# Where the scaling and the store of finished results stand around a value loop

## The chip, the cores and the metric

One core of a Trainium2 chip. The time is device microseconds of one execution; medians are over several executions on one chip. PE is the matrix engine, DVE the vector engine, ACT the scalar engine; SP issues the loads. A DMA has landed at the last of the 16 counts that the trace shows for it on its semaphore.

## The reference

Attention of one query a head over 4096 keys, for 8 x 32 heads of width 128, in bf16:

```python
scores = jnp.einsum('bhqd,bhkd->bhqk', q, k) * q.shape[-1] ** -0.5   # Sq = 1, Skv = 4096
attn = softmax(scores)
return jnp.einsum('bhqk,bhkd->bhqd', attn, v)
```

K and V are 268 MB each and are read once: 537 MB of loads against 0.07 MB of results.

## The kernel before

Eight heads make a tile, 32 tiles in all. A tile's K and V are 8.39 MB each and share three slots of SBUF. DVE multiplies K by the query and adds halves (lines 185, 188, 193), PE sums further against an identity (205), DVE reduces to scores (217), ACT takes exps (249), and PE multiplies the weights with V in a loop of its own (first and last matmuls line 274, the turns 288). ACT copies that result (344), PE folds it into `op` (360). In every second tile `op` is scaled by ACT (369), and after every fourth scaling a 16 KB store goes out from ACT (375). The loads are issued from SP (151).

```python
OB = 4          # results in one store
LOOP = 6        # matmuls in a turn of the value loop
kv_pool = ctx.enter_context(tc.tile_pool(name="kv_pool", bufs=SLOTS))   # SLOTS = 3
...
def values_loop(t):
    ...
    with tc.tile_critical() as loop:
        for i in range(EDGE): one(i, start=(i == 0), stop=False)        # L274
        with pe.While(...):
            for i in range(LOOP): pe.matmul(av, ...)                    # L288
            pe.reg_add(rw, rw, LOOP * nw); pe.reg_add(rv, rv, LOOP * nv)
        for i in range(NV - EDGE, NV): one(i, start=False, stop=(i == NV - 1))
    loops.append(loop)
...
def finish_of(n):
    s, u = divmod(n, OB)
    ...
    nc.scalar.activation(out=stages[s][:, u, :], in_=ops.pop(n)[:], func=ACT.Copy,
                         scale=rzs.pop(n)[:, 0:1])                      # L369
    last = s == NQ // OB - 1
    if u == OB - 1 or (last and u == OB - 2):
        lo = u if (last and u == OB - 1) else 0
        nc.scalar.dma_start(o_n[s, :, lo : u + 1, :], stages[s][:, lo : u + 1, :])   # L375
...
for t in range(NT):
    ...
    product(t, 0, Q);          sum_over_d(t, 0)
    ...
    product(t, Q, 2 * Q);      sum_over_d(t, 1);  scores_of(t, 0)
    product(t, 2 * Q, 3 * Q);  sum_over_d(t, 2);  scores_of(t, 1)
    if t > 2 and t % R == 1:
        recip_of(n)
        finish_of(n)
    product(t, 3 * Q, C);      sum_over_d(t, 3);  scores_of(t, 2)
    if loop:                                   # tiles 1 to 29
        values_loop(t - 1)
        load("k", t + 1);  load("v", t)
    ...
    scores_of(t, 3);  weights_of(t)
    if t > 0:
        copy_of(t - 1)
        ...
        result_of(t - 1)
```

The value loop is a section that is entered as a whole. In the trace of this kernel PE waits, ahead of the loop's first matmul, not only for the weights and V that it reads: in tiles 9, 17 and 25 its instruction records there wait on 13 semaphores, all eight that the DMAs count among them, and so the store's too. The wait on the store's semaphore was over at 402.09, 718.60 and 1035.73 us, 0.02 to 0.03 us behind the store's landing (402.06, 718.58, 1035.71), and the loop's first matmul had waited 10.25, 5.06 and 5.54 us.

Of the kernel before, what the change touches and what calls it, by code (L numbers as in the profile page):

```python
# [16 lines left out]
R = 2  # L17
OB = 4
# [7 lines left out]
def kernel(  # L26
# [7 lines left out]
    nc = tc.nc  # L34
# [15 lines left out]
    NQ = NT // R  # L50
# [95 lines left out]
    def load(kind, t):  # L146
        src = k_t if kind == "k" else v_t
        buf = kv_pool.tile([P, C, D], BF16, name=f"{kind}t", tag="kv")
        c0 = 0
        for n in cuts.get((kind, t), [C]):  # L150
            dma = nc.sync.dma_start(buf[:, c0 : c0 + n, :], src[t, :, c0 : c0 + n, :])
            behind_loop(dma)
            c0 += n
            if kind == "k" and t == 0 and c0 == n:
                nc.sync.dma_start(q_all[:], q_n)
        assert c0 == C
        loads[kind, t] = buf
# [3 lines left out]
    def q_prep(t):  # L161
        x, p0 = divmod(t * G, P)
        qh = ps_q.tile([G, D], F32, name="qh", tag="qp")
        nc.tensor.matmul(  # L164
            qh[:], lhsT=ident[:, p0 : p0 + G], rhs=q_all[:, x, :], start=True, stop=True
        )
        qg = q_pool.tile([G, D], BF16, name="qg", tag="qg")
        nc.scalar.activation(out=qg[:], in_=qh[:], func=ACT.Copy)  # L168
        qp = ps_q.tile([P, D], F32, name="qp", tag="qp")
        nc.tensor.matmul(qp[:], lhsT=heads[:].rearrange("g h x -> g (h x)"), rhs=qg[:], start=True, stop=True)  # L170
        qb = q_pool.tile([P, 1, D], BF16, name="qb", tag="qb")
        nc.scalar.activation(out=qb[:, 0, :], in_=qp[:], func=ACT.Copy)  # L172
        qbs[t] = qb
# [6 lines left out]
    def product(t, lo, hi):  # L180
        kt = loads["k", t]
        qb = qbs[t]
        for c0 in range(lo, hi, MC):
            part = kt[:, c0 : c0 + MC, :]
            nc.vector.tensor_tensor(  # L185
                out=part, in0=part, in1=qb[:].to_broadcast([P, MC, D]), op=ALU.mult
            )
            nc.vector.tensor_tensor(  # L188
                out=part[:, :, 0 : D // 2], in0=part[:, :, 0 : D // 2],
                in1=part[:, :, D // 2 : D], op=ALU.add,  # L190
            )
            if width_of(t, c0 // UC) < D // 2:
                nc.vector.tensor_tensor(  # L193
                    out=part[:, :, 0 : D // 4], in0=part[:, :, 0 : D // 4],
                    in1=part[:, :, D // 4 : D // 2], op=ALU.add,
                )
# [3 lines left out]
    def sum_over_d(t, u):  # L200
        kt = loads["k", t]
        ps = ps_s.tile([P, UC, DS], F32, name="ps", tag="ps")
        n = width_of(t, u) // DS
        for s in range(n):
            nc.tensor.matmul(  # L205
                ps[:], lhsT=ident[:],
                rhs=kt[:, u * UC : (u + 1) * UC, s * DS : (s + 1) * DS],
                start=(s == 0), stop=(s == n - 1),
            )
        sums[t, u] = ps  # L210
# [3 lines left out]
    def scores_of(t, u):  # L214
        if u == 0:
            scs[t] = sc_pool.tile([P, C], F32, name="sc", tag="sc")
        made = nc.vector.tensor_reduce(  # L217
            out=scs[t][:, u * UC : (u + 1) * UC], in_=sums.pop((t, u))[:], axis=AX.X, op=ALU.add
        )
        if u == NU - 1:  # L220
            behind_loop(made)
# [4 lines left out]
    def weights_of(t):  # L226
        sc = scs.pop(t)
        pmax = small.tile([P, 1], F32, name="pmax", tag="pmax")
        nc.vector.tensor_reduce(out=pmax[:], in_=sc[:], axis=AX.X, op=ALU.max)  # L229
        spread = small.tile([P, TB], F32, name="spread", tag="spread")  # L230
        nc.vector.tensor_scalar(  # L231
            out=spread[:], in0=same[:], scalar1=pmax[:, 0:1], scalar2=-scale,
            op0=ALU.add, op1=ALU.mult,
        )
        nmax = small.tile([P, 1], F32, name="nmax", tag="nmax")
        nc.vector.tensor_reduce(  # L236
            out=nmax[:], in_=spread[:], axis=AX.X, op=ALU.min, apply_transpose=True
        )
        bias = small.tile([P, G], F32, name="bias", tag="bias")
        nc.vector.tensor_scalar(  # L240
            out=bias[:], in0=own[:], scalar1=nmax[:, 0:1], scalar2=None, op0=ALU.add
        )
        w = w_pool.tile([P, C // CB, G, CB], BF16, name="w", tag="w")
        if t % R == 0:
            esums[t // R] = small.tile([P, R, G], F32, name="esum", tag="esum")
        esum = esums[t // R]
        sc_g = sc[:].rearrange("p (i m) -> p i m", m=CB)
        for g in range(G):
            nc.scalar.activation(  # L249
                out=w[:, :, g, :], in_=sc_g, func=ACT.Exp, bias=bias[:, g : g + 1], scale=scale,  # L250
                accum_out=esum[:, t % R, g : g + 1],
            )
        ws[t] = w
        if t == NT - 1:
            nc.gpsimd.tensor_copy(
                out=w_last[:, :, RG - G : RG].rearrange("p m g -> p g m"),
                in_=w[:, (C - LAST) // CB, :, :],
            )
# [67 lines left out]
    def norm_of(n):  # L326
        zp = ps_z.tile([RG, 1], F32, name="zp", tag="zp")
        nc.tensor.matmul(
            zp[:], lhsT=esums.pop(n).rearrange("p r g -> p (r g)"), rhs=ones[:],
            start=True, stop=True,  # L330
        )
        zps[n] = zp

    def recip_of(n):
        rzs[n] = small.tile([RG, 1], F32, name="rz", tag="rz")
        nc.vector.reciprocal(out=rzs[n][:], in_=zps.pop(n)[:])  # L336
# [3 lines left out]
    def copy_of(t):  # L340
        comb = o_pool.tile([P, CB, D], BF16, name="comb", tag="comb")
        av = avs.pop(t)[:].rearrange("p (m d) -> p m d", d=D)
        n = AG if t < LT else P
        nc.scalar.activation(out=comb[0:n, :, :], in_=av[0:n, :, :], func=ACT.Copy)  # L344
        combs[t] = comb
# [19 lines left out]
    def finish_of(n):  # L365
        s, u = divmod(n, OB)
        if u == 0:
            stages[s] = o_pool.tile([RG, OB, D], BF16, name="stage", tag="stage")
        nc.scalar.activation(  # L369
            out=stages[s][:, u, :], in_=ops.pop(n)[:], func=ACT.Copy, scale=rzs.pop(n)[:, 0:1]  # L370
        )
        last = s == NQ // OB - 1
        if u == OB - 1 or (last and u == OB - 2):
            lo = u if (last and u == OB - 1) else 0
            nc.scalar.dma_start(o_n[s, :, lo : u + 1, :], stages[s][:, lo : u + 1, :])  # L375
# [5 lines left out]
    with tc.manual_schedule(engines={E.PE, E.DVE, E.Activation, E.SP}):  # L381
        q_prep(0)
        for t in range(NT):
            loop = 0 < t <= LT
            v_last = t >= NT - 2
            n = t // R - 1
            if not loop:
                if t + 1 < NT:
                    load("k", t + 1)
                load("v", t)  # L390
            product(t, 0, Q)
            sum_over_d(t, 0)
            if t + 1 < NT:
                q_prep(t + 1)
            product(t, Q, 2 * Q)
            sum_over_d(t, 1)
            scores_of(t, 0)
            product(t, 2 * Q, 3 * Q)
            sum_over_d(t, 2)
            scores_of(t, 1)  # L400
            if t > 2 and t % R == 1:
                recip_of(n)
                finish_of(n)
            product(t, 3 * Q, C)
            sum_over_d(t, 3)
            scores_of(t, 2)
            if loop:
                values_loop(t - 1)
                load("k", t + 1)
                load("v", t)  # L410
            if v_last:
                values_of(t - 1, 0, C)
            scores_of(t, 3)
            weights_of(t)
            if t > 0:
                copy_of(t - 1)
                if t % R == 0:
                    norm_of(n)
                result_of(t - 1)
        values_of(NT - 1, 0, C // 2)  # L420
        norm_of(NQ - 1)
        recip_of(NQ - 1)
        values_of(NT - 1, C // 2, C - LAST)
        copy_of(NT - 1)
        result_of(NT - 1)
        finish_of(NQ - 1)


# [28 lines left out]
```

## Time and profile before

| | before |
|---|---|
| median of 3 runs | 1283.41 us (1279.34 to 1284.44) |
| span of the profiled run | 1280.6 us |
| loads' packets, share of 16 DMA engines | 98.0% |
| DVE, PE busy | 81%, 60% |
| stores that stand ahead of a value loop | 3 (tiles 9, 17, 25) |
| these stores, from issue to landing | 19.0, 14.0, 14.6 us |

The DMA share of 98.0% says that the loads are nearly the limit here. It does not say what the missing 2% are. In the list of issues on SP, the distance from one K load to the next gives the time of a tile: where it is longer than its neighbours, the trace holds a stall, and the waits of the engines at that time give its cause. The prediction shows these views.

### The profile page before, as it was taken

Reading aid. Unit: us, or ns where it says so; the run is one execution under the profiler, and the core shown is the slowest. Engines: PE = TensorE matmul, PEld = TensorE weight load, DVE = VectorE, ACT = ScalarE, POOL = GpSimd, SP = SyncE. Lnnn points to the kernel's source line nnn. Section 1 sums busy time; section 2 is a strip of 40 time slices with the busy share of each in tenths; the row PEclk is TensorE's granted clock in tenths of the full one; section 3 lists DMA queues with packets and bytes.
Section 4 is the critical chain, followed back from the end, with each engine's and each line's share of the span. In section 5 each row is a group of like instructions: output and inputs, shape, how many; then the busy total and the mean of one; then the engine's idle time right before and its main releaser. Section 6 shows DMA issues by size and latency. Waiting matters only on the chain. (4 is left out here: it accounts for less than half of the span.)

```text
span 1280.6 us, 11028 instructions
## 1 busy us (share of the span) xinstructions
PE 766.2 (60%) x3067; PEld 287.8 (22%) x3067; DVE 1040.6 (81%) x588; ACT 172.4 (13%) x625; POOL 3.3 (0%) x18
## 2 busy tenths in 40 slices
PE   2265567655574556765557655577555665557756
PEld 0021122221221122222222222222221222222222
DVE  5997888888986788888898787987889869788784
ACT  0111011111011101111101111111110111101111
POOL 0000000000000000000000000000000000000000
PEclk9577888777886788877788677887778877788867
DMA  9999999999999899999999999999999999999997
GB/s 426 428 393 426 428 424 441 414 434 428 440 430 396 356 430 414 426 428 437 426 426 437 416 393 426 422 428 439 416 436 434 432 402 394 426 426 427 428 447 304
DMA packets 11433, 537.33 MB, mean 420 GB/s; under 512 B 1808, under 2 KB 2064, under 8 KB 2320
## 3 DMA queue, kind: packets, MB, share of 16 engines
q1 hardware_dynamic: 11072, 536.94, 98.0%
q8 instruction: 14, 0.23, 0.1%
q10 hardware_dynamic: 336, 0.07, 0.0%
q14 instruction: 11, 0.09, 0.0%
HBM read 536.94 MB, written 0.07 MB: 419 GB/s over the span
## 5 line engine op out<-in xcount | busy, mean ns | idle before, releaser
L185 DVE TENSOR_TENSOR kt<-kt,qb 128x8192 bf16<-128x8192 bf16 x128 | 565.2, 4416 | 70.0 <-DMA kt<-in_k_dram 58.5
L205 PE MATMUL ps<-kt,ident 128*128 128x512 bf16 x792 | 261.0, 480 | 419.9 <-DVE kt L193 369.7
L288 PE MATMUL av<-vt,w 128*32 x1740 | 426.5, 397 | 4.7
L188 DVE TENSOR_TENSOR kt<-kt 128x4096 bf16<-128x4096 bf16 x128 | 293.4, 2292 | 4.4
L288 PEld LDWEIGHTS av<-vt,w 128*32 x1740 | 173.0, 99 | 263.9 <-issue 123.2
L205 PEld LDWEIGHTS <-ident 128*128 128x128 bf16 x792 | 84.5, 113 | 571.2 <-issue 523.2
L217 DVE TENSOR_REDUCE sc<-ps 128x64 f32<-128x512 f32 x128 | 88.0, 687 | 140.8 <-PE ps L205 140.8
L249 ACT ACTIVATE w<-sc,bias 128x256 bf16<-128x256 f32 x256 | 126.4, 494 | 518.5 <-DVE bias L240 518.5
L193 DVE TENSOR_TENSOR kt<-kt 128x2048 bf16<-128x2048 bf16 x58 | 71.0, 1225 | 2.0
L274 PE MATMUL av<-vt,w 128*32 128x512 bf16 x116 | 47.3, 501 | 34.0 <-DMA out_dram<-stage 15.8
L344 ACT ACTIVATE comb<-av 32x512 bf16<-32x512 f32 (+1 forms) x32 | 18.8, 587 | 345.2 <-PEq L278 337.5
L249 ACT ACTIVATION_READ_ACCUMULATOR w<-sc,bias 128x1 f32 x256 | 47.7, 186 | 0.0
L360 PE MATMUL op<-comb,pick 32*16 32x128 bf16 (+1 forms) x128 | 12.1, 213 | 25.8 <-ACT comb L344 25.8
L274 PEld LDWEIGHTS av<-vt,w 128*32 128x32 bf16 x116 | 7.1, 101 | 74.1 <-issue 73.7
L369 ACT ACTIVATE stage<-op,rz 16x128 bf16<-16x128 f32 x16 | 5.7, 358 | 132.4 <-DVE rz L336 132.0
L168 ACT ACTIVATE qg<-qh 8x128 bf16<-8x128 f32 x32 | 8.5, 267 | 99.4 <-PE qh L164 99.4
L360 PEld LDWEIGHTS <-pick 32*16 32x16 bf16 (+1 forms) x128 | 8.8, 83 | 32.9 <-issue 32.5
L316 PE MATMUL av<-vt,w 128*32 128x512 bf16 x191 | 15.4, 418 | 0.0
L164 PE MATMUL qh<-q_all,ident 128*8 128x128 bf16 x32 | 7.1, 221 | 13.1 <-DMA q_all<-in_q_dram 13.1
L229 DVE TENSOR_REDUCE pmax<-sc 128x1 f32<-128x256 f32 x32 | 13.4, 420 | 1.1
L170 PE MATMUL qp<-qg,heads 8*128 8x128 bf16 x32 | 6.8, 213 | 11.4 <-ACT qg L168 11.4
L172 ACT ACTIVATE qb<-qp 128x128 bf16<-128x128 f32 x32 | 8.9, 278 | 9.6 <-PE qp L170 9.6
(29 smaller groups left out, 47.9 us busy)
## 6 DMA issues: line engine op xcount, KB each, us to landing
kt<-in_k_dram SPq DMA_DIRECT2D x7, 4096.0 KB, 21.2
kt<-in_k_dram SPq DMA_DIRECT2D x2, 2048.0 KB, 15.2
vt<-in_v_dram SPq DMA_DIRECT2D x1, 4096.0 KB, 32.1
vt<-in_v_dram SPq DMA_DIRECT2D x1, 2048.0 KB, 36.6
vt<-in_v_dram SPq DMA_DIRECT2D x1, 1024.0 KB, 38.7
vt<-in_v_dram SPq DMA_DIRECT2D x1, 512.0 KB, 38.2
vt<-in_v_dram SPq DMA_DIRECT2D x31, 24.1
kt<-in_k_dram SPq DMA_DIRECT2D x28, 26.4
```

Source lines behind the costliest of these rows:

```text
L185: nc.vector.tensor_tensor(out=part, in0=part, in1=qb[:].to_broadcast([P, MC, D]), op=ALU.mult)
L188: nc.vector.tensor_tensor(out=part[:, :, 0 : D // 2], in0=part[:, :, 0 : D // 2], in1=part[:, :, D // 2 : D], op=ALU.add,)
L193: nc.vector.tensor_tensor(out=part[:, :, 0 : D // 4], in0=part[:, :, 0 : D // 4], in1=part[:, :, D // 4 : D // 2], op=ALU.add,)
L205: nc.tensor.matmul(ps[:], lhsT=ident[:], rhs=kt[:, u * UC : (u + 1) * UC, s * DS : (s + 1) * DS], start=(s == 0), stop=(s == n - 1),)
L217: made = nc.vector.tensor_reduce(out=scs[t][:, u * UC : (u + 1) * UC], in_=sums.pop((t, u))[:], axis=AX.X, op=ALU.add)
L229: nc.vector.tensor_reduce(out=pmax[:], in_=sc[:], axis=AX.X, op=ALU.max)
L249: nc.scalar.activation(out=w[:, :, g, :], in_=sc_g, func=ACT.Exp, bias=bias[:, g : g + 1], scale=scale, accum_out=esum[:, t % R, g : g + 1],)
L274: pe.matmul(av, lhsT=wf[:, i * nw : (i + 1) * nw], rhs=vf[:, i * nv : (i + 1) * nv], **how)
L288: pe.matmul(av, lhsT=wf[:, bass.ds(ow + i * nw, nw)], rhs=vf[:, bass.ds(ov + i * nv, nv)], start=False, stop=False,)
L316: nc.tensor.matmul(avs[t][j * AG : (j + 1) * AG, :], lhsT=w[:, i, :, :], rhs=vt[:, c0 : c0 + CB, :], start=(i < TG), stop=(j not in group[ ...
L344: nc.scalar.activation(out=comb[0:n, :, :], in_=av[0:n, :, :], func=ACT.Copy)
L360: nc.tensor.matmul(ops[n][:], lhsT=pick[0:e, m, r, :], rhs=comb[0:e, m, :], start=(r == 0 and m == 0), stop=(r == R - 1 and m == CB - 1),)
```

## The change

The intent: a store must not stand in the way of the value loop. Scaling goes behind the exps of the tile and so behind the loop in the program; the store goes behind the copy of the loop's result.

```diff
-        nc.scalar.activation(
+        made = nc.scalar.activation(
             out=stages[s][:, u, :], in_=ops.pop(n)[:], func=ACT.Copy, scale=rzs.pop(n)[:, 0:1]
         )
+        behind_loop(made)
+
+    def store_of(n):
+        s, u = divmod(n, OB)
         last = s == NQ // OB - 1
 ...
             if t > 2 and t % R == 1:
                 recip_of(n)
-                finish_of(n)
             product(t, 3 * Q, C)
 ...
             weights_of(t)
+            if t > 2 and t % R == 1:
+                finish_of(n)
             if t > 0:
                 copy_of(t - 1)
+                if t > 2 and t % R == 1:
+                    store_of(n)
 ...
         finish_of(NQ - 1)
+        store_of(NQ - 1)
```

## The prediction

> **What bounds the kernel now.** I read the page first, for the load queue; then the order of the load issues; then, where that order breaks, who waits for whom; last the neighbourhood of one break in time.
>
> The page says that the loads are the resource in use nearly all the time, while DVE is 81% and PE 60% busy:
>
> ```profile
> PE 766.2 (60%) x3067; PEld 287.8 (22%) x3067; DVE 1040.6 (81%) x588; ACT 172.4 (13%) x625; POOL 3.3 (0%) x18
> ...
> q1 hardware_dynamic: 11072, 536.94, 98.0%
> ```
>
> That alone would say "nothing on ACT can matter". But 98.0% of 1280.6 us leaves some 26 us, and it is worth asking where they lie. The issues of loads on the SP queue, in time order (K and V of a tile alternate), around the seventh to eleventh tile:
>
> ```profile
> 331.59 0.33 SPq L151 DMA_DIRECT2D kt<-in_k_dram  x1
> 353.62 0.33 SPq L151 DMA_DIRECT2D vt<-in_v_dram  x1
> 370.44 0.33 SPq L151 DMA_DIRECT2D kt<-in_k_dram  x1
> 392.53 0.33 SPq L151 DMA_DIRECT2D vt<-in_v_dram  x1
> 419.36 0.33 SPq L151 DMA_DIRECT2D kt<-in_k_dram  x1
> 441.32 0.33 SPq L151 DMA_DIRECT2D vt<-in_v_dram  x1
> 458.13 0.33 SPq L151 DMA_DIRECT2D kt<-in_k_dram  x1
> ```
>
> The normal distance from K to K is 38.9 us (370.44 - 331.59 = 38.85; 458.13 - 419.36 = 38.77). It is 22.0 us from K to V and 16.8 us from V to K. From 370.44 to 419.36 it is 48.92. In the whole list only two other distances stand out: 691.93 to 735.79 (43.86) and 1008.47 to 1053.01 (44.54). Over 38.9 these are 10.0, 5.0 and 5.6 us: 20.6 us in all, and no later tile catches up (458.13, 497.06, 536.01 go on at 38.8 to 39.0).
>
> What holds a K load is the end of the value loop, whose slot it takes; and the loop started late. The waits view gives PE's reasons:
>
> ```profile
> PE av L274 <- DMA out_dram<-stage: 15.8, 2, 10.2
> PE av L274 <- issue: 11.8, 27, 0.6
> ...
> PE av L274 <- DMA kt<-in_k_dram: 5.1, 1, 5.1
> ```
>
> 27 loops start 0.4 to 0.6 us after the matmuls ahead of them; three wait 10.2, 5.6 and 5.1 us. Two are put down to the store of the results. The third (at 719.04) is put down to a K load, but I hold it for the store too: in the trace the last part of that store landed at 718.58 and the K load at 718.78, and the list of waits in the built program has the store's semaphore ahead of that loop and not this K load's. In time:
>
> ```profile
> 383.10 7.00 ACTq L375 DMA_DIRECT2D out_dram<-stage  x1
> ...
> 390.63 1.86 PE L205 MATMUL ps<-kt,ident 128*128 128x512 bf16 x4 [6.71 <-DVE kt L193]
> ...
> 402.75 1.03 PE L274 MATMUL av<-vt,w 128*32 128x512 bf16 x2 [10.25 <-DMA out_dram<-stage]
> ...
> 422.25 0.69 DVE L217 TENSOR_REDUCE sc<-ps 128x64 f32<-128x512 f32 x1 [11.50 <-PE ps L205]
> ```
>
> PE is free at 392.5; the loop starts at 402.75; it ends at 419.4; behind it PE makes the sums that DVE then waits 11.5 us for (2.0 us in a usual tile, at 373.40). So the ring is: loop, sums on PE, DVE's products, sums, loop. It closes in 38.9 us and has no room, so a late loop is a late everything. The data queue runs dry meanwhile: 319 and 262 GB/s in 408 to 416 and 416 to 424 us, 426 to 434 usual.
>
> [...] the branch into each loop has a chain of such waits on all DMA semaphores, [...] the store included, though the loop reads nothing of it. [...] a 16 KB store is 80 packets, 5 on each of 16 engines, and a load packet takes 2.42 us; [...] the stores land 14.0 and 14.6 us after their issue (19.0 for the first, whose issue alone took 7.00). [...] Here 0.32 us of issue against 14 us to landing. [...] The packet records show a load of 8.39 MB ending every 19.34 us when the queue is full, 434 GB/s[...].
>
> **The change part by part.** Nothing is added or removed: PE, DVE and SP keep their order, and ACT only moves two things.
>
> Scaling (16 ACTIVATEs of 358 ns): from ahead of the loop to behind the eight exps of the same tile. In the loop tiles ACT then waits some 10 us for the loop's end (10.87 us idle ahead of the copy at 370.51), so 0.36 us there is hidden. In the last odd tile, which has no loop, the chain of waits runs exps (to 1268.66), copy, result: there 0.36 us is on the path. Cost +0.4.
>
> Stores (three of 16 KB in loop tiles): from ahead of the loop to behind the copy that follows it. The built program drops the store from that loop's counts[...]. Gain at the present loops: 10.0 + 5.0 + 5.6 = 20.6 us. The new deadline: counted from a V issue S, the loop ends at S + 16.8, the copy 0.65 later, so the store is issued at about S + 17.6 and lands at S + 31.6 to 32.2, or S + 36.6 if the first one again takes 7 us to issue. The next loop starts at S + 38.9 + 0.6 = S + 39.5. Margin 7 us, 2.9 us for the first: no wait.
>
> A 7 us issue on ACT would sit ahead of the query copy that PE waits for (373.55 in a usual tile): about 3.5 us late. PE's second sums end then at about K issue + 10.2, while DVE asks for them at K issue + 11.5 (381.93 - 370.44). Hidden, with 1.3 us to spare.
>
> What does not come back: the loads. With a full queue two loads cost 38.7 us at best, and in the undisturbed stretches K lands every 39.05 us (523.63 to 718.90 in five tiles) to 39.17 (840.24 to 1036.07), a little more than the ring's 38.9. DVE's wait for K grows from 0.54 us behind the first stall to 2.95 ahead of the second, and from 1.52 to 3.6 ahead of the third, while its wait for PE shrinks to 0.5 to 0.9. So the stalls gave the ring no slack but gave DVE slack against the loads. Without them the loads come to bind: up to 15 tiles at 0 to 0.2 us, some 1.5 us (estimate), and some 0.7 us more at the end, where the last V pieces have been only about 2 us ahead of their matmuls. Sum: -20.6 + 0.4 + 1.5 + 0.7 = -18.0 us. From the median of 1283.4 that is 1265.4; I say 1265.
>
> **The rivals.** (a) The wait moves: the store lands behind the start of the next loop. For it: [...] the 19.0 us landing leaves only 2.9 us. Against it: the two other landings leave 7. If only the first is late by some 3 us, 1268; if all three waits move whole, 1284. (b) The loads bind alone: the gain is only the load time lost. For it: 98.0% busy. Counting how much longer than 19.34 us each load at the three breaks took, from the packet records, gives 10.3 + 5.8 + 4.8 = 20.9 us, of which some 2 us are the usual spread (0.23 us a load): 18.8 us, so even then 1265. The two ways of counting agree, which narrows the range. (c) More than the stalls is won, say because loops at other odd tiles also waited for the scaling. Against it: they start as promptly as the rest, within 0.6 us. It would need 25.7 us to pass 2%, more than the three waits hold. (d) Nothing: the stores' wait overlapped a wait for data. Against it: no V landing stands near 402.75 or 1036.06, and the issue distances jump by the same amounts.
>
> **Range and chances.** The steps of the sum carry 2 to 3 us of doubt (loads), the first store 3, and the runs of the kernel before spread from 1279.3 to 1284.4. So 1261 to 1270. 2% would be 1257.7, beyond the 20.6 us on offer: faster 0.03; slower 0.02; within 2% 0.95.
>
> **What would show it.** Right: no K to K distance over 40 us but for the first tiles; no wait of the loop's first matmul over 1 us; issues of stores about 0.7 us behind the K issue; landings of 12 to 19 us; DVE waits for K that climb to about 4 us and stay, and a load queue near 99%. Wrong: a loop wait of some us one tile later, which names the store (rival a); or prompt loops with K to K distances of 39.3 and more (the loads took the gain). A median under 1261 would mean the loads keep up better than I read.

With the cuts goes the reason that it gave for landings of about 14 us; the landings themselves (19.0, 14.0 and 14.6 us) are measured, and the new deadline uses these alone. That the next loop waits for a store that now stands ahead of it was my assumption: the runs show such waits only for stores issued in the loop's own tile (the kernel before, `e2_early_ahead`, `e4_twice_ahead`, `e9_before_loop30`). What the text says of waits in the program can be seen in the traces. Ahead of the loop at 719.04 the wait on the store's semaphore was over at 718.60, behind its landing at 718.58, and the one on the K load's semaphore at 718.71, ahead of that load's landing at 718.78; so this K load was not what the loop waited for. In the changed kernel the loop at 392.92 starts ahead of the store's issue at 409.67.

## The result, and the profile after

| | before | after |
|---|---|---|
| median | 1282.97 us (4 runs, 1279.34 to 1284.44) | 1261.68 us (4 runs, 1261.61 to 1261.99) |
| ratio | | 0.9839 (95% interval 0.9818 to 0.9859) |
| span of the profiled run | 1280.6 us | 1260.2 us |
| K to K at tiles 9, 17, 25 | 48.92, 43.86, 44.54 us | 39.20, 38.97, 38.90 us |

A ratio is the mean time of one kernel's runs over that of the other's of the same rounds, so it is not quite the ratio of the medians quoted. The time of 1261.68 us lies in the range of 1261 to 1270, near its lower end, and within 2% of before.

The issues of loads after the change, on the SP queue, at the place where the stall of 10 us was:

```profile
370.32 0.33 SPq L151 DMA_DIRECT2D kt<-in_k_dram  x1
392.40 0.33 SPq L151 DMA_DIRECT2D vt<-in_v_dram  x1
409.52 0.33 SPq L151 DMA_DIRECT2D kt<-in_k_dram  x1
431.55 0.33 SPq L151 DMA_DIRECT2D vt<-in_v_dram  x1
448.35 0.33 SPq L151 DMA_DIRECT2D kt<-in_k_dram  x1
```

K to K is 39.20 and 38.83 us; V to K is 17.1 us at the place where it was 26.8. The same stretch on all engines, cut to the scaling, the loop, the copy and the store:

```profile
392.92 1.03 PE L274 MATMUL av<-vt,w 128*32 128x512 bf16 x2 [0.55 <-issue]
...
398.33 0.34 ACT L369 ACTIVATE stage<-op,rz 16x128 bf16<-16x128 f32 x1
...
409.59 0.59 ACT L344 ACTIVATE comb<-av 32x512 bf16<-32x512 f32 x1 [10.92 <-PEq L278]
409.67 0.40 ACTq L379 DMA_DIRECT2D out_dram<-stage  x1
...
412.47 0.69 DVE L217 TENSOR_REDUCE sc<-ps 128x64 f32<-128x512 f32 x1 [1.52 <-PE ps L205]
...
431.95 1.03 PE L274 MATMUL av<-vt,w 128*32 128x512 bf16 x2 [0.43 <-issue]
```

The loop starts at 392.92 instead of 402.75, DVE waits 1.52 us for the sums instead of 11.50, and the next loop, ahead of which the store now stands, starts 0.43 us after PE is free; the store landed at 423.76, 8.2 us before it. The scaling fills a piece of ACT's long wait for the loop's end.

The waits view after: DVE's two main waits, then the only line that is left of PE's waits shown in the prediction:

```profile
DVE sc L217 <- PE ps L205: 106.0, 61, 4.5
...
DVE kt L185 <- DMA kt<-in_k_dram: 72.6, 26, 3.9
...
PE av L274 <- issue: 13.4, 31, 0.6
```

No loop waits for a store any more. And DVE's two waits before:

```profile
DVE sc L217 <- PE ps L205: 140.8, 61, 11.5
...
DVE kt L185 <- DMA kt<-in_k_dram: 58.5, 23, 3.9
```

DVE waits 34.8 us less for PE and 14.1 us more for K. The sum is 20.7 us less, the size of the gain: DVE does the same work in a shorter time. The loads' share on the page rises:

```profile
q1 hardware_dynamic: 11072, 536.94, 99.1%
```

### The profile page after: what moved, and what is told of

Its sections match the earlier page's. It is cut to its first block, busy times and chain, and to the rows that moved or that the text cites. A ratio compares the mean times of both kernels' runs of the same rounds, so it can differ in the third digit from the quotient of the medians.

```text
span 1260.2 us, 11027 instructions
## 1 busy us (share of the span) xinstructions
PE 765.0 (61%) x3067; PEld 287.5 (23%) x3067; DVE 1040.8 (83%) x588; ACT 170.6 (14%) x625; POOL 3.3 (0%) x18
## 3 DMA queue, kind: packets, MB, share of 16 engines
q1 hardware_dynamic: 11072, 536.94, 99.1%
## 5 line engine op out<-in xcount | busy, mean ns | idle before, releaser
L185 DVE TENSOR_TENSOR kt<-kt,qb 128x8192 bf16<-128x8192 bf16 x128 | 565.2, 4416 | 84.0 <-DMA kt<-in_k_dram 72.6
L217 DVE TENSOR_REDUCE sc<-ps 128x64 f32<-128x512 f32 x128 | 88.0, 687 | 106.0 <-PE ps L205 106.0
L274 PE MATMUL av<-vt,w 128*32 128x512 bf16 x116 | 47.3, 500 | 14.7 <-issue 13.4
L229 DVE TENSOR_REDUCE pmax<-sc 128x1 f32<-128x256 f32 x32 | 13.5, 421 | 1.1
## 6 DMA issues: line engine op xcount, KB each, us to landing
vt<-in_v_dram SPq DMA_DIRECT2D x1, 512.0 KB, 39.2
```

The source lines that it names most:

```text
L185: nc.vector.tensor_tensor(out=part, in0=part, in1=qb[:].to_broadcast([P, MC, D]), op=ALU.mult)
L217: made = nc.vector.tensor_reduce(out=scs[t][:, u * UC : (u + 1) * UC], in_=sums.pop((t, u))[:], axis=AX.X, op=ALU.add)
L229: nc.vector.tensor_reduce(out=pmax[:], in_=sc[:], axis=AX.X, op=ALU.max)
L274: pe.matmul(av, lhsT=wf[:, i * nw : (i + 1) * nw], rhs=vf[:, i * nv : (i + 1) * nv], **how)
```

## The experiments

The theory: a loop starts late when a store that stands ahead of it in the program has not landed; the ring of loop, sums and products passes the whole delay on. The rivals: moving the scaling brought part of it; any store ahead of a loop costs; a store has a fixed latency; the loads, not the ring, set the pace. All ten kernels gave the right result. Each ratio is to runs of the kernel before on the same chip, in three batches on three chips (medians of the kernel before: 1281.18 us for the first four experiments, 1281.97 for the next four, and 1280.77 for the last two); times of different batches are compared with that in mind.

**Scaling ahead, store behind** (`e1_scale_ahead`), the changed kernel with scaling at its old place:

```diff
             if t > 2 and t % R == 1:
                 recip_of(n)
+                finish_of(n)
...
-            if t > 2 and t % R == 1:
-                finish_of(n)
...
-        behind_loop(made)
```

> Scaling stays ahead of the loop as in the kernel before; the store alone is moved behind the copy. Theory (only the store's landing held the loop): the whole gain, 1261 to 1263 us, no wait of a loop's first matmul over 1 us, and 0.2 to 0.4 us less at the end than the changed kernel because no scaling stands between the last exps and the copy. Rival (moving the scaling, whose semaphore every odd loop also waits for, brought part of the gain): 1265 to 1275 us.

Measured: 1261.99 us, ratio to before 0.9852 (0.9836 to 0.9868); no loop waits over 0.6 us:

```profile
PE av L274 <- issue: 12.9, 29, 0.6
```

The store alone carries the gain. The scaling's cost at the end is too small for the medians, but the traces show it: from the first of the last eight exps to the copy behind them it is 3.95 us here and in the kernel before, and 4.19 us in the changed kernel.

**Still ahead of the loop, but earlier** (`e2_early_ahead`), the kernel before with one move:

```diff
             scores_of(t, 0)
+            if t > 2 and t % R == 1:
+                recip_of(n)
+                finish_of(n)
             product(t, 2 * Q, 3 * Q)
...
-            if t > 2 and t % R == 1:
-                recip_of(n)
-                finish_of(n)
```

> The kernel before with reciprocal, scaling and store one product earlier: still ahead of the loop, but issued about 8.5 us sooner, some 18 us ahead of the loop's usual start instead of 9.9. Theory (what counts is whether the store lands before the loop starts; it takes about 14 us): 1261 to 1263 us, no loop waits, or one of up to 2 us if the first store again takes 7 us to issue. Rival (a store ahead of the loop costs its 5 us at the loop's entry wherever it stands): 1275 to 1283 us.

Measured: 1265.83 us, ratio 0.9882 (0.9866 to 0.9898). Two of the three waits are gone; the first is left, and larger than the 2 us that I had allowed. Its lines in order of time:

```profile
374.79 5.73 ACTq L375 DMA_DIRECT2D out_dram<-stage  x1
...
396.91 1.04 PE L274 MATMUL av<-vt,w 128*32 128x512 bf16 x2 [4.29 <-DMA kt<-in_k_dram]
```

Its issue again took long, and it needed 21.4 us from issue to landing: it landed at 396.2, 3 us behind the loop's usual start; K to K is 42.97 us there and 38.8 to 39.2 at the other tiles. One wait of 4.3 us on top of 1261.7 is about the 1265.8 measured. (The profile puts the wait down to a K load, as it did once in the kernel before. The last part of that K landed at 397.4, behind the loop's start, so it was not what the loop waited for.) The side of the loop does not matter; whether the store has landed does.

**Small stores ahead of every second loop** (`e3_small_ahead`), the kernel before with:

```diff
-        last = s == NQ // OB - 1
-        if u == OB - 1 or (last and u == OB - 2):
-            lo = u if (last and u == OB - 1) else 0
-            nc.scalar.dma_start(o_n[s, :, lo : u + 1, :], stages[s][:, lo : u + 1, :])
+        nc.scalar.dma_start(o_n[s, :, u : u + 1, :], stages[s][:, u : u + 1, :])
```

> The kernel before with one 4 KB store for each result tile (14 ahead of a loop, not 3), at the old place ahead of the loop. Theory ([...] a 4 KB store has 2 packets an engine instead of 5): landing 5 to 8 us after the issue, within the 9.9 us to the loop's start, so no loop waits over 1 us and 1261 to 1264 us. Rival (landing has a floor of 12 us or more under this load, whatever the size): 14 waits of some 4 us, 1310 to 1340 us.

Measured: 1262.33 us, ratio 0.9855 (0.9838 to 0.9871); the loops wait 0.6 us at most. Fourteen stores stand ahead of a loop and cost nothing, because they land in time. All stores of this run, least, median and most:

```profile
DMA to landing us min/median/max: 1.3/8.5/8.9
```

The landing is a little above the 5 to 8 us that I expected, an estimate, and under the 9.9 us that the loop leaves.

**Two stores for one** (`e4_twice_ahead`), the kernel before with:

```diff
             nc.scalar.dma_start(o_n[s, :, lo : u + 1, :], stages[s][:, lo : u + 1, :])
+            if not last:
+                nc.scalar.dma_start(o_n[s + 1, :, lo : u + 1, :], stages[s][:, lo : u + 1, :])
```

> The kernel before with each of the three 16 KB stores followed by a second one of the same size (into the next group's rows, which are overwritten later, so the result stays right). Theory [...] (10 store packets an engine instead of 5[...]): the second lands about 26 us after the issue, each loop waits some 12 us more than before, 1315 to 1325 us. Rival (fixed latency to HBM that two stores share): 1283 to 1287 us.

Measured: 1317.24 us, ratio 1.0283 (1.0266 to 1.03). PE's waits in this run; the second is the last of three, where an instruction of DVE happened to end near the landing:

```profile
PE av L274 <- DMA out_dram<-stage: 39.5, 2, 22.3
PE av L274 <- DVE kt L185: 16.9, 1, 16.9
```

The three loops wait 56.4 us instead of 20.9, that is 35.5 us more, and the time grows by 36.1 us. 80 packets more each time (576 in all on the stores' queue, against 336) cost some 12 us each time; a fixed latency would have cost nothing. The 26 us expected for the landing was an estimate of mine. With `e3_small_ahead` this gives three points for the landing beside full loads: 2 packets an engine, 8.2 to 8.9 us; 5 packets, 13.4 to 16.7 over all runs (without the stores whose issue took long); 10 packets, 24.1 to 25.3.

**A longer loop** (`e5_loop3`): the changed kernel with `LOOP = 3` for `LOOP = 6`, so with more turns.

> The changed kernel with three matmuls a turn of the value loop instead of six: 20 turns, not 10. At the full clock a turn's end costs some 0.23 us in the trace of the changed kernel (6 matmuls take 1.51 us, the matmuls alone 1.28), so a loop gets 1.3 to 2.3 us longer. Theory (the ring of loop, sums and products still sets the pace): every one of 28 tiles pays it, 1297 to 1325 us. Rival (the loads set the pace and the ring has slack): under 1270 us.

Measured: 1424.67 us, ratio 1.1113 (1.1096 to 1.113). The direction was right, the size was not: 163 us more, not 36 to 64. I had taken a turn's 0.23 us as a constant. In the trace of this run turns follow each other every 1.04 us where the matmuls in them are some 0.21 us apart, and nearly every turn's end shows. With six it was 1.51, but only about half of the ten ends show. So a turn's end costs 0.40 us behind three matmuls, and 0.23 or nothing behind six. A loop, from its first matmul to the end of its last, takes 21.95 us on average instead of 16.30, 5.65 more. K to K is 44.5 us, 5.6 more, and 29 loops make some 162 of the 163. So the ring of the changed kernel has no slack: DVE waits for PE, and for K no more, and the loads are far from their limit here:

```profile
DVE sc L217 <- PE ps L205: 343.4, 61, 12.4
...
q1 hardware_dynamic: 11072, 536.94, 90.1%
```

**A shorter loop** (`e6_loop30`): the changed kernel with `LOOP = 30`, so with two turns.

> The changed kernel with 30 matmuls a turn: 2 turns, a loop 1 to 1.8 us shorter. Theory (ring and loads are nearly level, 38.97 us a tile against 38.7 to 38.9 of load packets): the loads take over at once, so 1253 to 1261 us, DVE waits for K on every tile up to where PE no longer makes it wait. Rival (only the ring counts): 28 times 1 to 1.8 us, 1212 to 1234 us. Rival (the loads count already): 1261 to 1263 us.

Measured: 1255.88 us, ratio 0.9797 (0.9784 to 0.981). This is the fastest version, ahead of both kernels. The loads have taken over. DVE's two waits say so: more for K (72.6 us in the changed kernel), less for PE (106.0):

```profile
DVE kt L185 <- DMA kt<-in_k_dram: 101.9, 23, 5.5
...
DVE sc L217 <- PE ps L205: 57.6, 35, 4.0
```

K to K is now mostly twice 38.1 and then once 39.9 us, 38.7 on average, against 38.97 in the changed kernel and 38.68 for the packets of two loads back to back. Early on, while the loads still have room, a tile took 37.43 us, so the ring itself is some 1.5 us shorter; over the whole run only 0.2 to 0.3 us a tile is left of that.

**A shorter loop and K loads in halves** (`e7_kcut_loop30`):

```diff
-        for n in cuts.get((kind, t), [C]):
+        for n in cuts.get((kind, t), [C // 2] * 2 if kind == "k" else [C]):
```

> The same with every K load in two halves, so that DVE can start on a tile about 10 us before the whole of it is there. If the moment at which a whole K load lands holds the tile of the run with 30 matmuls a turn, this is faster than it by 1 us or more, down to the packets' own 38.7 us a tile: 1250 to 1256 us. If the packets' rate alone holds it: the same within 1 us. If the ring holds it: the same, and DVE's waits for K go.

Measured: 1258.35 us, ratio 0.9814 (0.9801 to 0.9828): 2.5 us slower than with whole loads, which none of my cases had. The tiles begin faster (37.5 us K to K over some ten tiles, while the ring sets the pace), then the loads' rate holds them as before (38.1 and 39.9). The last piece of V lands at 1251.8 us against 1250.0, and the end of the kernel behind it takes 5.0 us against 4.0. So the moment at which a whole K is there does not hold the tile; the rate does. Why the loads end later in the pieces was not looked into. The cut also changed the packets of these K loads from 64 to 32 KB, so there are more of them (11072 without it):

```profile
q1 hardware_dynamic: 15104, 536.94, 99.2%
```

**The store during the loop** (`e8_store_in_loop`), the changed kernel with the store right behind the scaling:

```diff
                 finish_of(n)
+                store_of(n)
             if t > 0:
                 copy_of(t - 1)
-                if t > 2 and t % R == 1:
-                    store_of(n)
```

> The changed kernel with the store right behind the scaling, issued some 5 us into the loop instead of at its end; in the program it still stands behind the loop. Theory (it matters only which loop's entry counts it, and the next one is 34 us off): 1261 to 1263 us and no loop wait. Rival (a store while the loop runs and K starts costs load time): 1264 us or more.

Measured: 1261.96 us, ratio 0.9845 (0.983 to 0.986). No difference: that the store stands behind the copy as well adds nothing that the medians show to its being behind the loop. (At the end its issue adds 0.5 us between the last exps and the copy: 4.69 us against 4.19.)

**The old place with the shorter loop** (`e9_before_loop30`): the kernel before with `LOOP = 30`.

> The kernel before, stores ahead of the loop, with 30 matmuls a turn. Against the run with 30 matmuls a turn and the stores moved (1255.88 us) it differs by the place of scaling and store alone, in a setting where the loads set the pace. Theory (a late loop leaves the load queue dry, and dry time is lost whoever sets the pace, less what a shorter loop gives back before the next load is due): 1266 to 1276 us. Rival (once the loads set the pace, the loop's wait hides behind them): 1256 to 1260 us.

Measured: 1268.92 us, ratio 0.9912 (0.9897 to 0.9927). Against 1255.88 the place of scaling and store is worth 13.0 us here (12.7 against `e10_loop15`, which ran on the same chip), though the loads set the pace. Its waits:

```profile
PE av L274 <- DMA out_dram<-stage: 16.8, 2, 10.3
...
PE av L274 <- DMA kt<-in_k_dram: 6.6, 1, 6.6
```

23.4 us of waits cost 13.0 us. The rest was probably covered by the room that a shorter ring has against the loads; behind each stall the tiles take 37.7 to 38.2 us for a while, less than the loads' 38.7, which fits.

**Four turns** (`e10_loop15`): the changed kernel with `LOOP = 15`.

> The changed kernel with 15 matmuls a turn, 4 turns. If with 30 a turn the loads alone set the pace, a loop that is some 0.5 us longer than that one's still fits: 1255 to 1258 us, K to K distances of 38.7 us on average. If the ring still counted there: 1261 us or more.

Measured: 1256.21 us, ratio 0.9807 (0.9793 to 0.982). As with 30. But the run is no test of a longer loop: I had expected one 0.5 us longer, and a loop takes 15.26 us on average against 15.21 with 30. In the trace the matmuls follow each other 0.22 us apart across the turns' ends, so behind 15 matmuls a turn's end costs nothing that shows.

## Why the prediction was right

*What bounds.* The ring was the bound, and the three late loops were its only breaks. Shown by `e5_loop3` (a loop 5.65 us longer makes a tile 5.6 us longer) and by the distances, which are even after the change.

*The store holds the loop.* Shown four ways: away from the loop's entry the waits vanish (`e1_scale_ahead`), earlier they vanish but for the store that was slow (`e2_early_ahead`), smaller they vanish (`e3_small_ahead`), doubled they grow by 35.5 us (`e4_twice_ahead`). The third wait, which the profile put down to a K load, went with the other two.

*The new deadline.* The store was to be issued 0.7 us behind K and land 7 us ahead of the next loop. It was issued 0.15 us behind K (in the lines above its issue starts at 409.67, while the copy ahead of it on ACT runs to 410.18), and landed in 13.5 to 14.1 us. The first one took 0.40 us to issue, not 7.00, so the 2.9 us margin was not needed. Rival (a) did not happen.

*The sum.* From trace to trace, 20.4 us:

| term | predicted | measured | from |
|---|---|---|---|
| three late loops | -20.6 | -20.25 | K to K at the three places, before less after |
| scaling on the path at the end | +0.4 | +0.25 | first of the last exps to the copy: 4.19 against 3.95 us |
| loads come to bind | +1.5 | +0.1 | K at 370 to the first issue of the last K: 817.35 us after, 837.46 - 20.25 before |
| loads at the end | +0.7 | -0.4 | from that issue to the end: 72.5 against 72.7 us, less the 0.25 |
| sum | -18.0 | -20.3 | |

The step that was mis-sized is the one on the loads. I read the growth of DVE's wait for K behind a stall (1.52 to 3.6 us) as a drift that goes on. It was the return to a usual level. The trace before could have told: ahead of the second stall the wait for K had levelled at 2.1 to 2.95 us, with DVE still waiting 1.9 us or more for PE, so the 0.5 to 0.9 us that I gave for the wait for PE hold ahead of the third stall alone. After the change the wait for K does not climb to 4 us and stay: it is 2.2 to 3.9 us over 17 tiles, PE still makes DVE wait 0.65 us or more in each, and DVE's starts on a landed K are 39.01 us apart (397.54 to 1060.71) against 38.97 for the ring. The loads came close and did not bind; `e6_loop30` shows how close, since a shorter ring ran into them at 38.7 us. Medians differ by 21.3 us rather than 20.4 because the profiled run of the kernel before (1282.37 us) lies 0.6 us under its median, and that of the changed kernel (1261.99) 0.3 us over.

*Rival (b)*, the loads alone, gave 1265 by another count and so looked like support. As the bound of the changed kernel it is refuted by `e5_loop3`: there all of the loop's added time comes through. The kernel before was further from that bound (DVE waited 58.5 us for K, against 72.6).

## What to carry to other kernels

Here a section that is entered as a whole waited up to 10.25 us for a store that it does not read, because the store stood ahead of it in the program; so place such slow things behind its entry (1261.68 us) or early enough to land (1262.33 us with small stores). In these runs a store beside large loads landed the later the more packets it had: 8.2 to 8.9 us with 2 an engine, 13.4 to 16.7 with 5, 24.1 to 25.3 with 10. Its bytes grew along, and the runs do not part the two, but at the loads' 434 GB/s 16 KB would take 0.04 us (an estimate), not 14. In a kernel whose DMA is 98% busy, look for the places where the regular distance between loads breaks: the small rest may be a few stalls with a cause of their own, and once they are gone the next bound is near (here 6 us further on).

## What else the traces show

- Beside load packets of 64 KB and 2.42 us each (kernel before), a store of 2 packets an engine landed in 8.2 to 8.9 us (`e3_small_ahead`), of 5 in 13.4 to 16.7, the second of two such stores in 24.1 to 25.3 (`e4_twice_ahead`).
- This program on one core loaded 8.39 MB every 19.34 us, 434 GB/s, when the queue was full (kernel before).
- The end of a turn of the loop on PE, with its register steps, cost 0.40 us behind three matmuls (`e5_loop3`), 0.23 us or nothing behind six (changed kernel), and nothing that shows behind 15 or 30 (`e10_loop15`, `e6_loop30`).
- The issue of the first 16 KB store from ACT took 7.00, 5.73, 7.02 and 5.90 us in four traces (before, `e2_early_ahead`, `e4_twice_ahead`, `e9_before_loop30`) and 0.40 us in the changed kernel. In the kernel before an 8 KB packet of the instruction queue lies within the issue (at 388.4 us); in the changed kernel that packet came at 376.1, well ahead of the store at 409.7. No run tested whether the two belong together.
